# A delta rule, a PReLU MLP and a SwiGLU MLP on one core: a new order for the parts of gh, for the inverse products and for the decoding of weights

## The chip, the cores and the metric

One core of a Trainium2 chip. The time is the device time of one execution in microseconds (us): before, 1178.39, 1181.08 and 1181.10 us in three runs (median 1181.08). The profiled execution, from which all rows come, took 1177.41 us, with a span of 1175.7 us between its first and last instruction.

The engines are TensorE (PE in the rows, its weight loads PEld), VectorE (DVE), ScalarE (ACT), GpSimd (POOL) and SyncE (SP), which issues the DMAs.

## What is computed

```python
# attention: q, k, v (4, 8, 768, 48), beta (4, 8, 768)
k_n = k / (norm(k) + 1e-06)
for t in range(768):
    y[t]  = q[t] @ state
    v_old = state @ k_n[t]
    state = state + beta[t] * outer(k_n[t], v[t] - v_old)
x = y as (3072, 384)
# first MLP, PReLU
h = x @ w_in                                  # 384 -> 2048
g = maximum(h, 0) + alpha * minimum(h, 0)
x = g @ w_out                                 # 2048 -> 384
# second MLP, SwiGLU
out = (silu(x @ w_gate) * (x @ w_val)) @ w_out2   # 384 -> 1536 -> 384
```

Inputs and outputs are float32, but `w_in`, `w_out`, `w_gate` and `w_val` come as float64 and are read as 64-bit words.

## The kernel before

**Arithmetic.** Every large product is made in three passes: both factors are split into a high part (a copy in the fp32r format of TensorE) and a low part (the value less its high part), and high by high, high by low and low by high are summed. A high part is a copy by ScalarE; a low part is a subtraction on VectorE or GpSimd.

**Weights.** The 64-bit words of a slice of 128x384 weights are turned into float32 by four instructions: a scaled read of the upper words by ScalarE (`act`, tile `wf`, L518), and three bit operations on VectorE (`dve(0)` to `dve(2)`, L526, L528, L532). Then `split` makes the high part on ScalarE (L539) and the low part (L540). The first MLP has 32 slices, 16 of `w_in` and 16 of `w_out` by turns; the generator `all_w1` (called `conv`) decodes them, three steps for each slice, during the prelude and the first block. In its order, slice i+1 is read by ScalarE ahead of the bit operations of slice i, and both parts of slice i-1 are made at the second step of slice i. Odd slices have their low part on VectorE, even ones on GpSimd. `wf` has three buffers.

**Attention.** The 768 positions are 24 chunks of 32, in 6 windows of 4 chunks, with all 32 heads together. A window needs the inverse of a triangular 32x32 matrix for each head and chunk, in two halves of 16 (`lanes` for the later windows, `lanes2` for the first; HC is 16): a long elimination on VectorE, then for each pair of chunks (z = 0 and 1) a product `out1(z)` (L342), a copy out of PSUM by ScalarE into `tmp`, a second product (L364) and a subtraction into `TT`. The recurrence over chunks has the steps QS, KS, U, S, Y and XT; XT turns a chunk's result into columns of x, `xh` and `xl`.

**First MLP.** 12 blocks (n) of 256 tokens, 16 hidden slices (j). `H1(n, j)` is nine matmuls (L599), then two relus on ScalarE (L609, L610, tile `pn`), the PReLU sum on VectorE (L612), the high part of g on ScalarE (L616, tile `gh`) and its low part on GpSimd (L617). `O1(n, j)` is nine matmuls (L628) that add to a PSUM tile `o`; behind the last j of a block, ScalarE (L638) and VectorE (L643) copy `o` into `xs`, which goes to DRAM. `o` has one buffer, so that O1(n+1, 0) waits for these copies.

**Second MLP.** 8 blocks of 384 tokens (L686, L696 to L702, L715). Its weights are decoded early, stored in DRAM, and read again; their splits (`make_w2`), two in each step, and the first `split_x2` (L670, L671) lie in block 11 of the first MLP.

**Order.** Nothing is scheduled by a program: `manual_schedule` keeps the order in which the code is written. `prelude()` is straight code, in which `go(inv, k)` and `go(conv, k)` advance the inversion and the decoding by k steps. After it comes a list of events, each with a time u by which they are sorted; one unit is one H1. H1(n, j) is at 16n + j, O1(n, j) at 16n + j + 2.5. Each engine works its own instructions off in this order and waits where an operand isn't there or a buffer isn't free.

Of the kernel before, what the change touches and what calls it, by code (L numbers as in the profile page):

```python
# [13 lines left out]
AF = mybir.ActivationFunctionType  # L14
ALU = mybir.AluOpType
# [9 lines left out]
def kernel(  # L25
# [25 lines left out]
    nc = tc.nc  # L51
# [13 lines left out]
    NB1 = NCH // 2  # L65
    NB2 = NCH // CB2
    LA = 2
    W64 = 1
    WF = 3

    dram = ctx.enter_context(tc.tile_pool(name="dram", bufs=1, space=bass.MemoryType.DRAM))
    x2d = [dram.tile([128, 2, NK, 128], F32, name=f"x2d{n}") for n in range(NB1)]
# [2 lines left out]
    ws = ctx.enter_context(tc.tile_pool(name="ws", bufs=2 * J1))  # L75
# [169 lines left out]
    HC = C // 2  # L245
# [56 lines left out]
    def lanes2(w, early=False):  # L302


        t = Lanes(w)
        t.new_X()
        t.turn(0)
        yield
        t.turn(1)
        yield  # L310
        t.norm()
        t.length(0)
        yield
        Lv = free_view(t.L, 0, [[HC * C + HC, 2], [C, HC], [1, HC]])
        av = free_view(t.a, 0, [[HC, 2], [1, HC], [0, HC]])
        nc.vector.tensor_tensor(Lv, Lv, av, ALU.mult)
        yield
        tv = t.new("tmp", "tmp", [128, 512])
        B2 = [HC * C + HC, 2]
        for i in range(HC - 1):  # L320
            n, m = HC - 1 - i, i + 1
            v = free_view(tv, 0, [[n * m, 2], [m, n], [1, m]])
            Xv = free_view(t.X, (i + 1) * C, [B2, [C, n], [1, m]])
            Lc = free_view(t.L, (i + 1) * C + i, [B2, [C, n], [0, m]])
            Xr = free_view(t.X, i * C, [B2, [0, n], [1, m]])
            nc.vector.tensor_tensor(v, Lc, Xr, ALU.mult)
            t.length(2 * i + 1)
            nc.vector.tensor_tensor(Xv, Xv, v, ALU.subtract)
            t.length(2 * i + 2)
            yield  # L330
        Dm = t.new("Dm", "lane", [128, 32, C], 2)
        nc.gpsimd.memset(Dm[:, :, HC:C], 0.0)
        TT_t[w] = t.new("TT", "TT", [128, 32, C], 2)
        t.turn_X(1)
        G, TT = GL.pop(w), TT_t[w]
        ps = [None, None]

        def out1(z):
            ps[z] = bank(early, "pi")
            for y in range(HC * z, HC * z + HC):  # L340
                for b in range(4):
                    nc.tensor.matmul(  # L342
                        ps[z][rows(b), (y % HC) * HC:(y % HC) * HC + HC],
                        G[rows(b), y, :],
                        TT[rows(b), y, HC:C],
                        start=True,
                        stop=True,
                        skip_group_check=True,
                    )

        N = HC * HC
        uv = t.new("tmp", "tmp", [128, 512])
        t.turn_Dm(Dm)
        yield
        for z in range(2):
            out1(z)
            nc.scalar.activation(out=uv[:, z * N:z * N + N], in_=ps[z][:, 0:N], func=AF.Copy)
            if z == 0:
                t.turn_X(0)
            yield  # L360
            for y in range(HC * z, HC * z + HC):
                for b in range(4):
                    r = slice(32 * b, 32 * b + HC)
                    nc.tensor.matmul(  # L364
                        ps[z][rows(b), N + (y % HC) * HC:N + (y % HC) * HC + HC],
                        Dm[r, y, :],
                        uv[r, y * HC:y * HC + HC],
                        start=True,
                        stop=True,
                        skip_group_check=True,  # L370
                    )
            Tv = TT[:, HC * z:HC * z + HC, HC:C]
            nc.vector.tensor_tensor(
                Tv, Tv, ps[z][:, N:2 * N].rearrange("p (y i) -> p y i", y=HC), ALU.subtract
            )
            yield

    LANES2 = 4 + HC - 1 + 6
# [115 lines left out]
    class Slice:  # L494
# [8 lines left out]
        def load(self, eng=nc.sync):  # L503
# [3 lines left out]
            else:  # L507
                if self.home is None:
                    w = wstg.tile([128, 384], I64, name="w64", tag="w64", bufs=W64)
                else:  # L510
# [25 lines left out]
    def split(f, eng, pool, tag):  # L536

        t = pool.tile([128, 2, 384], F32R, name="w", tag=tag, **({} if pool is ws else dict(bufs=1)))
        nc.scalar.activation(out=t[:, 0], in_=f, func=AF.Copy)  # L539
        eng.tensor_tensor(t[:, 1], f, t[:, 0], ALU.subtract)  # L540
        return t

    def w_cols(w, j):
        return w[:, j * 128:j * 128 + 128].rearrange("(k p) f -> p k f", p=128)
# [4 lines left out]
    w1 = []  # L549
# [7 lines left out]
    w1_s = [w1_slice(i) for i in range(2 * J1)]  # L557

    w2 = {}
    w2_order = [(j, z) for j in range(J2) for z in range(3)]  # L560
    w2d, w2_s = {}, {}
# [20 lines left out]

    def make_w2(i):
        pool, tag = (ws, "w") if i < 2 * J1 else (P2["x"], f"w{i}")
        w2[w2_order[i]] = split(w2_s.pop(i), nc.gpsimd if i % 2 else nc.vector, pool, tag)

    PASSES = ((0, 0), (0, 1), (1, 0))

# [1 line left out]
    g1_t, o1_t = {}, {}  # L590

    def H1(n, j):
        ps = ps_h1.tile([128, 512], F32, name="h1", tag="h1")
        w = w1[2 * j]
        x = x1_t[n]
        i = 0
        for kk in range(NK):
            for a, b in PASSES:
                nc.tensor.matmul(  # L599
                    ps[:, 0:N1],  # L600
                    w[:, a, kk * 128:kk * 128 + 128],
                    x[b][:, kk, :],
                    start=(i == 0),
                    stop=(i == 3 * NK - 1),
                )
                i += 1
        hv = ps[:, 0:N1]
        pn = g1.tile([128, 2, N1], F32, name="pn", tag="pn", bufs=2)
        nc.scalar.activation(out=pn[:, 1], in_=hv, func=AF.Relu, scale=-1.0)  # L609
        nc.scalar.activation(out=pn[:, 0], in_=hv, func=AF.Relu)  # L610
        g = pn[:, 0]
        nc.vector.scalar_tensor_tensor(  # L612
            out=g, in0=pn[:, 1], scalar=nalpha[:, j:j + 1], in1=pn[:, 0], op0=ALU.mult, op1=ALU.add
        )
        gh = g1.tile([128, 2, N1], F32R, name="gh", tag="gh", bufs=3)
        nc.scalar.activation(out=gh[:, 0], in_=g, func=AF.Copy)  # L616
        nc.gpsimd.tensor_tensor(gh[:, 1], g, gh[:, 0], ALU.subtract)  # L617
        g1_t[n, j] = gh
# [45 lines left out]
    def split_x2(n):  # L664
        r = x2r_t.pop(n).rearrange("p c k t -> p k c t")
        t = P2["x"].tile([128, 2, NK, N2], F32R, name="x2s", tag="x2s")
        hv = t[:, 0].rearrange("p k (c t) -> p k c t", c=CB2)
        lv = t[:, 1].rearrange("p k (c t) -> p k c t", c=CB2)
        for kk in range(NK):
            nc.scalar.activation(out=hv[:, kk], in_=r[:, kk], func=AF.Copy)  # L670
            nc.gpsimd.tensor_tensor(lv[:, kk], r[:, kk], hv[:, kk], ALU.subtract)  # L671
        x2_t[n] = t

    u2_t, o2_t = {}, {}
# [61 lines left out]
    def at(u, fn, *args):  # L736
        events.append((u, len(events), fn, args))
# [10 lines left out]
    def load_w1(*slices, eng=nc.sync):  # L748
        for i in slices:
            w1_s[i].load(eng)  # L750

    def all_w1():

        n = 2 * J1
        w1_s[0].act()
        for i in range(n):
            if i + 1 < n:
                w1_s[i + 1].act()
            for z in range(3):
                w1_s[i].dve(z)  # L760
                if z == 1 and i > 0:
                    make_w1(i - 1)
                yield
        make_w1(n - 1)
        yield

    def make_w1(i):
        w1.append(split(w1_s[i].f, nc.vector if i % 2 else nc.gpsimd, ws, "w"))

    conv = all_w1()  # L770

    def go(g, n=1):
        for _ in range(n):
            next(g, None)
# [4 lines left out]
    def prelude():  # L779
# [10 lines left out]
        for g in range(4):  # L790
            m = mask[32 * g:32 * g + 32, :]
            nc.gpsimd.affine_select(
                out=m, in_=m, pattern=[[1, C]], compare_op=ALU.is_gt, fill=0.0, base=0, channel_multiplier=-1
            )
        load_nat(0, "k", nat)
        load_w1(0, 1)
        load_beta(0, nc.gpsimd)
        load_v(0, nc.gpsimd)
        load_v(1, nc.gpsimd)
# [1 line left out]
        n = 0  # L801
# [2 lines left out]
                pre_T(0, "k", b1, half, nat, early=n % 2 == 1, eng="act" if n % 2 == 0 else "dve")  # L804
                n += 1
        load_nat(0, "q", natq0)
        load_w1(2, 3)
        load_nat(1, "k", nat)
        nc.sync.dma_start(out=alpha_r, in_=moe_alpha.rearrange("(j p) -> j p", p=128))
        load_k2(0)  # L810
# [6 lines left out]
        inv = lanes2(0, True)  # L817
        go(inv, 3)
        n = 0
# [56 lines left out]
    def base(c):  # L876
        return {4: 20, 5: 25.7}.get(c, 8 * (c - 2))

    CONV_DONE, CONV_END = 41, 14.0
    CONV_N = 3 * 2 * J1 + 1 - CONV_DONE  # L880
    for i in range(CONV_N):
        at(-0.5 + i * CONV_END / CONV_N, go, conv)
# [1 line left out]
    for w in range(1, NWIN):  # L884
        P = base(4 * w) - 32
        if w == 1:
# [4 lines left out]
            l0, l1, n = 6.6, 18.5, LANES  # L891
        else:
# [9 lines left out]
            l0, l1, n = P + 15, P + 31.5, LANES  # L902
# [22 lines left out]
    for n in range(NB1):  # L925
        for j in range(J1):
            at(16 * n + j, H1, n, j)
            at(16 * n + j + LA + 0.5, O1, n, j)
    if WIDE2:
        NW2 = len(w2_order)  # L930

# [30 lines left out]
    for i in late:  # L962
        at(E1 - 16 + 3 + i / 2, fetch_w2, i)
        at(E1 - 16 + 5.1 + i / 2, make_w2, i)
    at(E1 + LA + 0.6, end1)
    for n in range(NB2):
        u = E1 + LA + 1 + J2 * n
        at(max(u - 10, E1 - 1.1) if n else E1 - 10, load_x2, n)
# [39 lines left out]
```

## Time and profile before

| | |
|---|---|
| runs | 1178.39, 1181.08, 1181.10 us |
| profiled execution | 1177.41 us (span 1175.7 us) |
| TensorE busy | 1087.1 us, 92% of the span |
| VectorE busy | 621.9 us, 53% |
| ScalarE busy | 444.4 us, 38% |
| GpSimd busy | 330.4 us, 28% |
| HBM traffic | 57.52 MB read, 16.52 MB written, 63 GB/s |

The span has these stages: the prelude with the first chunks of the recurrence, up to the first relu of H1(0, 0) at 73.8 us; block 0 of the first MLP with the rest of the weight decoding, up to 157.4; blocks 1 to 10, up to 665.3; block 11, up to 712; and the second MLP, up to the end. The average share of each engine hides that different engines are full in different stages, so the rows are read stage by stage. In a row of the timeline the number in brackets at the end is how long the engine was idle just before, and what ended it; "issue" is time in which it waited for nothing that the profile shows. A start is counted from the span's start. Matmuls overlap in part, so that a group's time is a little longer than the distance to the next.

### The profile page before, as it was taken

Reading aid. Unit: us, or ns where it says so; the run is one execution under the profiler, and the core shown is the slowest. Engines: PE = TensorE matmul, PEld = TensorE weight load, DVE = VectorE, ACT = ScalarE, POOL = GpSimd, SP = SyncE. Lnnn points to the kernel's source line nnn. Section 1 sums busy time; section 2 is a strip of 40 time slices with the busy share of each in tenths; the row PEclk is TensorE's granted clock in tenths of the full one; section 3 lists DMA queues with packets and bytes.
Section 4 is the critical chain, followed back from the end, with each engine's and each line's share of the span. In section 5 each row is a group of like instructions: output and inputs, shape, how many; then the busy total and the mean of one; then the engine's idle time right before and its main releaser. Section 6 shows DMA issues by size and latency. Waiting matters only on the chain.

```text
span 1175.7 us, 37218 instructions
## 1 busy us (share of the span) xinstructions
PE 1087.1 (92%) x16125; PEld 1049.6 (89%) x16125; DVE 621.9 (53%) x1313; ACT 444.4 (38%) x1158; POOL 330.4 (28%) x517
## 2 busy tenths in 40 slices
PE   6678689899999999999999989999999999999996
PEld 5567689889989998998899979999999999999996
DVE  6578963794497379449744255333333333333332
ACT  3254344335435543543444564222222222222221
POOL 4133732463274246327433373101010101001000
PEclk8579779999999999999999999999999999999998
DMA  9562021234224323422222153010101010101000
GB/s 224 166 203 44 2 68 39 76 83 123 57 82 107 86 74 83 119 61 70 78 76 76 56 155 101 1 42 1 41 1 41 1 41 1 41 4 38 11 11 20
DMA packets 140080, 76.44 MB, mean 65 GB/s; under 512 B 104000, under 2 KB 134624, under 8 KB 139916
## 3 DMA queue, kind: packets, MB, share of 16 engines
q1 hardware_dynamic: 139340, 73.45, 22.9%
q8 instruction: 126, 2.06, 0.7%
q0 software_dynamic: 576, 0.61, 0.2%
q14 instruction: 38, 0.31, 0.1%
HBM read 57.52 MB, written 16.52 MB: 63 GB/s over the span
## 4 chain that ended last, share of the span: by engine, by line
PE 60%; DVE 19%; issue 13%; ACT 3%; POOL 2%; DMA 1%; POOLq 0%; DVEq 0%; SPq 0%; ACTq 0%
PE gv L686 21%; PE o L715 10%; PE o L628 10%; PE h L599 10%; DVE tmp L257 4%; DVE pn L612 3%; DVE X L265 2%; PE pg L167 2%; DVE wf L532 1%; PE pt L148 1%; PE pst L444 1%; PE py L465 1%; DVE wf L528 1%; PE pk L400 1%; POOL w L540 1%
## 5 line engine op out<-in xcount | busy, mean ns | idle before, releaser
L686 PE MATMUL gv<-x2s,w 128*128 128x384 f32 x1728 | 317.8, 336 | 0.0
L686 PEld LDWEIGHTS gv<-x2s,w 128*128 128x128 f32 x1728 | 304.3, 188 | 0.0
L628 PE MATMUL o<-gh,w 128*128 128x256 f32 x1728 | 258.2, 293 | 22.8 <-POOL gh L617 9.6
L599 PE MATMUL h<-xh,w 128*128 128x256 f32 x1152 | 243.6, 288 | 12.7 <-ACT pn L610 6.7
L628 PEld LDWEIGHTS o<-gh,w 128*128 128x128 f32 x1728 | 223.1, 193 | 35.6 <-POOL gh L617 13.7
L617 POOL TENSOR_TENSOR gh<-pn,gh 128x256 fp32r<-128x256 f32 x192 | 151.7, 790 | 341.3 <-ACT gh L616 307.1
L599 PEld LDWEIGHTS h<-xh,w 128*128 128x128 f32 x1152 | 195.8, 194 | 15.7 <-ACT pn L610 7.3
L612 DVE SCALAR_TENSOR_TENSOR pn<-pn,nalpha 128x256 f32<-128x256 f32 x192 | 100.2, 522 | 150.6 <-ACT pn L610 149.5
L599 PE MATMUL h<-xl,w 128*128 128x256 f32 x576 | 165.3, 287 | 2.7 <-DVE xl L491 2.7
L715 PE MATMUL o<-w,us 128*128 128x384 f32 x864 | 165.4, 337 | 0.0
L616 ACT ACTIVATE gh<-pn 128x256 fp32r<-128x256 f32 x192 | 80.2, 418 | 220.0 <-DVE pn L612 220.0
L715 PEld LDWEIGHTS o<-w,us 128*128 128x128 f32 x864 | 151.2, 188 | 0.0
L698 DVE TENSOR_TENSOR sg<-sg,gv 128x384 f32<-128x384 f32 x96 | 53.2, 554 | 175.9 <-ACT sg L696 175.9
L671 POOL TENSOR_TENSOR x2s<-x2r,x2s 128x384 fp32r<-128x384 f32 x24 | 24.2, 1037 | 333.8 <-ACT x2s L670 333.8
L599 PEld LDWEIGHTS h<-xl,w 128*128 128x128 f32 x576 | 112.0, 194 | 4.0 <-DVE xl L491 4.0
L701 ACT ACTIVATE us<-u 128x384 fp32r<-128x384 f32 x96 | 50.6, 527 | 165.0 <-DVE u L699 165.0
L696 ACT ACTIVATE sg<-gv 128x384 f32<-128x384 f32 x96 | 47.2, 491 | 169.7 <-PE gv L686 169.7
L609 ACT ACTIVATE pn<-h 128x256 f32<-128x256 f32 x192 | 72.5, 377 | 90.7 <-PE h L599 87.7
L702 DVE TENSOR_TENSOR us<-u,us 128x384 fp32r<-128x384 f32 x96 | 53.7, 559 | 62.8 <-ACT us L701 62.8
L699 DVE TENSOR_TENSOR u<-sg,gv 128x384 f32<-128x384 f32 x96 | 53.2, 554 | 45.7 <-PE gv L686 45.5
L610 ACT ACTIVATE pn<-h 128x256 f32<-128x256 f32 x192 | 72.9, 380 | 0.0
L257 DVE TENSOR_TENSOR tmp<-L,X 128x31 f32<-128x31 f32 (+29 forms) x155 | 65.7, 424 | 1.4
(101 smaller groups left out, 1047.9 us busy)
## 6 DMA issues: line engine op xcount, KB each, us to landing
w<-in_moe_w_out_dram SPq DMA_DIRECT2D x28, 384.0 KB
w2d<-wf SPq DMA_DIRECT2D x36, 192.0 KB
wf<-w2d SPq DMA_DIRECT2D x36, 192.0 KB
w<-in_moe_w_in_dram SPq DMA_DIRECT2D x16, 384.0 KB
nat<-in_k_dram SPq DMA_DIRECT2D x24, 192.0 KB
k<-in_k_dram SPq DMA_DIRECT2D x96, 48.0 KB
x2d<-xs SPq DMA_DIRECT2D x12, 384.0 KB
w<-in_moe_w_gate_dram SPq DMA_DIRECT2D x12, 384.0 KB
```

The source lines that it names most:

```text
L257: eng.tensor_tensor(w, t.L[:, i + 1:C, i:i + 1].to_broadcast([128, n, m]), t.X[:, i:i + 1, c0:c0 + m].to_broadcast([128, n, m]), ALU.mult,)
L599: nc.tensor.matmul(ps[:, 0:N1], w[:, a, kk * 128:kk * 128 + 128], x[b][:, kk, :], start=(i == 0), stop=(i == 3 * NK - 1),)
L609: nc.scalar.activation(out=pn[:, 1], in_=hv, func=AF.Relu, scale=-1.0)
L610: nc.scalar.activation(out=pn[:, 0], in_=hv, func=AF.Relu)
L612: nc.vector.scalar_tensor_tensor(out=g, in0=pn[:, 1], scalar=nalpha[:, j:j + 1], in1=pn[:, 0], op0=ALU.mult, op1=ALU.add)
L616: nc.scalar.activation(out=gh[:, 0], in_=g, func=AF.Copy)
L617: nc.gpsimd.tensor_tensor(gh[:, 1], g, gh[:, 0], ALU.subtract)
L628: nc.tensor.matmul(o[:, dm // 2, (dm % 2) * N1:(dm % 2) * N1 + N1], w[:, a, dm * 128:dm * 128 + 128], g[:, b], start=(j == 0 and i == 0 an ...
L686: nc.tensor.matmul(p[:, 0:N2], w2[j, z][:, a, kk * 128:kk * 128 + 128], x[:, b, kk], start=(i == 0), stop=(i == 3 * NK - 1),)
L698: nc.vector.tensor_tensor(sg, sg, ps[0], ALU.mult)
L702: nc.vector.tensor_tensor(us[:, 1], u, us[:, 0], ALU.subtract)
L715: nc.tensor.matmul(o2_t[n][t][:, 0:DM], us[:, a, t * 128:t * 128 + 128], w[:, b, :], start=(j == 0 and i == 0), stop=(j == J2 - 1 and i == 2),
```

## The change

There are five edits.

1. `all_w1`: ScalarE's read `act` goes two slices ahead instead of one, so `wf` has four buffers. The high part of slice i-1 stands at the first step of slice i, the low part at the second (both stood at the second). Low parts of odd slices below 16 (`W1_DVE`) move from VectorE to GpSimd: eight subtractions. In the prelude the third weight load stands ahead of the load of q, not behind it.
2. `lanes2`: `tmp` is 256 wide and is allocated for each z, and the prelude's `go` counts list the second pair of chunks (z = 1) behind XT(1), both products, instead of its first product ahead of U(0).
3. H1 is cut in two: the high and low part of g (`H1_parts`) are listed at 16n + j + 0.45, half a step behind the relus and the sum.
4. O1(n, 0) of blocks 1 to 11 is listed at 16n + 3.1 instead of 16n + 2.5.
5. The low parts of the first `split_x2` (three subtractions) are on VectorE instead of GpSimd.

```diff
-        tv = t.new("tmp", "tmp", [128, 512])
+        tv = t.new("tmp", "tmp", [128, 256])
...
-        uv = t.new("tmp", "tmp", [128, 512])
...
             out1(z)
-            nc.scalar.activation(out=uv[:, z * N:z * N + N], in_=ps[z][:, 0:N], func=AF.Copy)
+            uv = t.new("tmp", "tmp", [128, N])
+            nc.scalar.activation(out=uv, in_=ps[z][:, 0:N], func=AF.Copy)
...
         nc.scalar.activation(out=t[:, 0], in_=f, func=AF.Copy)
-        eng.tensor_tensor(t[:, 1], f, t[:, 0], ALU.subtract)
-        return t
+        return t, lambda: eng.tensor_tensor(t[:, 1], f, t[:, 0], ALU.subtract)
...
+    def H1_parts(n, j):
+        g = g1_t[n, j]
         gh = g1.tile([128, 2, N1], F32R, name="gh", tag="gh", bufs=3)
         nc.scalar.activation(out=gh[:, 0], in_=g, func=AF.Copy)
...
-            nc.gpsimd.tensor_tensor(lv[:, kk], r[:, kk], hv[:, kk], ALU.subtract)
+            eng = nc.gpsimd if n else nc.vector
+            eng.tensor_tensor(lv[:, kk], r[:, kk], hv[:, kk], ALU.subtract)
...
         n = 2 * J1
-        w1_s[0].act()
-        for i in range(n):
-            if i + 1 < n:
-                w1_s[i + 1].act()
+        rest = None
+        for i in range(-2, n + 1):
+            if i + 2 < n:
+                w1_s[i + 2].act()
+            if i < 0:
+                continue
             for z in range(3):
-                w1_s[i].dve(z)
-                if z == 1 and i > 0:
-                    make_w1(i - 1)
-                yield
-        make_w1(n - 1)
-        yield
-
-    def make_w1(i):
-        w1.append(split(w1_s[i].f, nc.vector if i % 2 else nc.gpsimd, ws, "w"))
+                if i < n:
+                    w1_s[i].dve(z)
+                if z == 0 and i > 0:
+                    t, rest = split(w1_s[i - 1].f, nc.vector if i >= W1_DVE and i % 2 else nc.gpsimd, ws, "w")
+                    w1.append(t)
+                if z == 1 and rest:
+                    rest()
+                if i < n or z == 1:
+                    yield
...
-        load_w1(0, 1)
+        load_w1(0, 1, 2)
...
-        load_w1(2, 3)
+        load_w1(3)
...
-        go(inv, LANES2 - 13 - 4)
+        go(inv, 7)
         go(inv)
         go(conv, 4)
         go(inv)
-        go(conv, 2)
+        go(conv, 3)
         do_QS(0)
         do_U(0)
...
             at(16 * n + j, H1, n, j)
-            at(16 * n + j + LA + 0.5, O1, n, j)
+            at(16 * n + j + 0.45, H1_parts, n, j)
+            at(16 * n + j + LA + (1.1 if j == 0 and n > 0 else 0.5), O1, n, j)
```

What stands where on the engines, at the three places that matter most. First TensorE in the prelude, before, from the warm-up matmuls to chunk 0's part of the recurrence (L342 and L364 are the two products of the inverse, L426 is U, L444 is S, L400 and L465 are QS, KS and Y):

```order
L746 MATMUL warm<-ident 96x96 x6
L342 MATMUL pi<-TT,GL 32x16 x64
L364 MATMUL pi<-tmp,Dm 32x16 x64
L342 MATMUL pi<-TT,GL 32x16 x64
L426 MATMUL pu<-v,TT 32x48 x32
L444 MATMUL pst<-U,k_105 64x48 x32
L400 MATMUL pk<-St,kqt 32x48 x32
```

The same place in the changed kernel, where the numbers of lines are one higher:

```order
L752 MATMUL warm<-ident 96x96 x6
L343 MATMUL pi<-TT,GL 32x16 x64
L365 MATMUL pi<-tmp,Dm 32x16 x64
L427 MATMUL pu<-v,TT 32x48 x32
L445 MATMUL pst<-U,k_105 64x48 x32
L401 MATMUL pk<-St,kqt 32x48 x32
```

The second group of 64 first products is gone from the place ahead of U(0). Further down the same engine, around XT(1) (L487) and ahead of the transposes of q (L148) and the first H1 (L599), stood:

```order
L465 MATMUL py<-U,mt 32x48 x32
L444 MATMUL pst<-U,k_105 64x48 x32
L487 MATMUL px<-ident,ys 128x128 x3
L364 MATMUL pi<-tmp,Dm 32x16 x64
L148 MATMUL pt<-ident,nat_103 128x128 x8
L148 MATMUL pt<-ident,nat_104 128x128 x8
L599 MATMUL h_1334<-xh,w 128x256
```

and now, in the changed kernel:

```order
L466 MATMUL py<-U,mt 32x48 x32
L445 MATMUL pst<-U,k_105 64x48 x32
L488 MATMUL px<-ident,ys 128x128 x3
L343 MATMUL pi<-TT,GL 32x16 x64
L365 MATMUL pi<-tmp,Dm 32x16 x64
L149 MATMUL pt<-ident,nat_103 128x128 x8
L149 MATMUL pt<-ident,nat_104 128x128 x8
L600 MATMUL h_1337<-xh,w 128x256
```

The 64 first products came here, directly ahead of the second ones, with ScalarE's copy into `tmp` between the two. Third, ScalarE in block 11, before, two steps (relus of one H1, high part of g, high parts of two slices of the second MLP's weights):

```order
L609 ACTIVATE pn<-h_12572 128x256
L610 ACTIVATE pn<-h_12572 128x256
L616 ACTIVATE gh<-pn 128x256
L539 ACTIVATE w<-wf_12513 128x384
L539 ACTIVATE w<-wf_12527 128x384
L609 ACTIVATE pn<-h_12608 128x256
```

and in the changed kernel:

```order
L610 ACTIVATE pn<-h_12573 128x256
L611 ACTIVATE pn<-h_12573 128x256
L540 ACTIVATE w<-wf_12511 128x384
L621 ACTIVATE gh<-pn 128x256
L540 ACTIVATE w<-wf_12528 128x384
L610 ACTIVATE pn<-h_12609 128x256
```

One of the two weight copies moved from behind `gh` to between the relus and `gh`.

## Rows read from the trace of the kernel before

**Rows 1.** Windows by stage: us, busy and count by engine, PEclk, DMA share, GB/s
```profile
core 0: us, PE busy (x) PEld busy (x) DVE busy (x) ACT busy (x) POOL busy (x), PEclk, DMA share, GB/s
0.00:73.80 73.80, 45.69 (x1622) 40.83 (x1622) 46.74 (x117) 29.75 (x76) 20.79 (x37) 0.70 0.80 221
73.80:105.00 31.20, 28.98 (x718) 26.85 (x719) 23.30 (x47) 17.56 (x47) 10.70 (x12) 0.84 0.33 76
105.00:157.40 52.40, 35.47 (x473) 31.43 (x472) 49.41 (x109) 17.69 (x48) 30.86 (x57) 0.71 0.01 2
157.40:665.30 507.90, 485.20 (x10439) 461.42 (x10439) 310.16 (x710) 233.54 (x673) 210.56 (x353) 0.99 0.30 79
665.30:712.00 46.70, 39.09 (x288) 36.75 (x287) 25.07 (x32) 29.30 (x82) 31.31 (x33) 0.95 0.49 146
712.00:1175.70 463.70, 452.69 (x2593) 452.34 (x2591) 167.26 (x301) 116.60 (x237) 26.21 (x27) 0.99 0.07 23
```

**Rows 2.** Timeline of TensorE in the prelude: start, us, instructions, idle before
```profile
41.49 1.62 PE L342 MATMUL pi<-TT,GL 32*32 32x16 f32 x106 [4.29 <-issue]
...
63.60 1.78 PE L364 MATMUL pi<-tmp,Dm 16*32 16x16 f32 x116 [2.45 <-issue]
...
69.41 0.37 PE L599 MATMUL h<-xh,w 128*128 128x256 f32 x1
```

**Rows 3.** Timeline of the weight decoding on VectorE, ScalarE and POOL
```profile
50.87 0.99 POOL L540 TENSOR_TENSOR w<-wf,w 128x384 fp32r<-128x384 f32 x1 [5.80 <-ACT w L539]
50.88 1.40 DVE L532 SCALAR_TENSOR_TENSOR wf<-w,wf 128x384 int32<-128x384 int32 x1
51.90 0.55 ACT L518 ACTIVATE wf<-w 128x384 f32<-128x384 f32 x1 [1.10 <-POOL w L540]
...
73.89 0.56 DVE L540 TENSOR_TENSOR w<-wf,w 128x384 fp32r<-128x384 f32 x1 [1.88 <-ACT w L539]
74.83 0.55 DVE L532 SCALAR_TENSOR_TENSOR wf<-w,wf 128x384 int32<-128x384 int32 x1
```

**Rows 4.** Windows of two stretches of block 0, columns as in Rows 1
```profile
75.50:85.70 10.20, 9.13 (x163) 8.14 (x166) 7.15 (x15) 5.10 (x13) 4.57 (x5) 0.50 0.20 45
85.80:113.00 27.20, 24.38 (x641) 22.47 (x629) 21.70 (x42) 13.64 (x36) 9.40 (x11) 1.00 0.24 47
```

**Rows 5.** One block's window, TensorE's waits (157.4:712, then 575:712), one timeline row
```profile
318.00:356.00 38.00, 34.30 (x733) 32.31 (x732) 35.33 (x82) 14.39 (x43) 25.41 (x51) 1.00 0.37 96
...
PE o L628 <- DVE xs L643: 6.7, 9, 1.4
...
PE o L628 <- DVE xs L643: 1.9, 3, 1.3
...
327.82 1.32 PE L628 MATMUL o<-gh,w 128*128 128x256 f32 x9 [1.39 <-DVE xs L643]
```

**Rows 6.** Timeline of block 11, and ScalarE's waits there (total us, times, longest)
```profile
675.98 1.21 PE L628 MATMUL o<-gh,w 128*128 128x256 f32 x9
...
678.08 1.21 PE L628 MATMUL o<-gh,w 128*128 128x256 f32 x9
...
684.67 0.42 ACT L616 ACTIVATE gh<-pn 128x256 fp32r<-128x256 f32 x1 [1.04 <-DVE pn L612]
685.00 0.92 ACT L539 ACTIVATE w<-wf 128x384 fp32r<-128x384 f32 x2
686.00 1.19 POOL L540 TENSOR_TENSOR w<-wf,w 128x384 fp32r<-128x384 f32 x1
686.56 0.91 DVE L612 SCALAR_TENSOR_TENSOR pn<-pn,nalpha 128x256 f32<-128x256 f32 x1 [0.25 <-ACT pn L610]
687.50 0.42 ACT L616 ACTIVATE gh<-pn 128x256 fp32r<-128x256 f32 x1 [1.04 <-DVE pn L612]
...
694.34 3.49 POOL L671 TENSOR_TENSOR x2s<-x2r,x2s 128x384 fp32r<-128x384 f32 x3
...
699.84 1.87 PE L628 MATMUL o<-gh,w 128*128 128x256 f32 x8 [1.99 <-POOL gh L617]
...
ACT gh L616 <- DVE pn L612: 15.4, 16, 1.3
```

More of the change, by code (lines that the diff above doesn't have):

```diff
@@ L67 @@
     LA = 2
+    W1_DVE = 16
     W64 = 1
-    WF = 3
+    WF = 4
     dram = ctx.enter_context(tc.tile_pool(name="dram", bufs=1, space=bass.MemoryType.DRAM))
@@ L366, in lanes2 @@
                         Dm[r, y, :],
-                        uv[r, y * HC:y * HC + HC],
+                        uv[r, (y % HC) * HC:(y % HC) * HC + HC],
                         start=True,
@@ L584, in make_w2 @@
         pool, tag = (ws, "w") if i < 2 * J1 else (P2["x"], f"w{i}")
-        w2[w2_order[i]] = split(w2_s.pop(i), nc.gpsimd if i % 2 else nc.vector, pool, tag)
+        w2[w2_order[i]], rest = split(w2_s.pop(i), nc.gpsimd if i % 2 else nc.vector, pool, tag)
+        rest()
     PASSES = ((0, 0), (0, 1), (1, 0))
@@ L614, in H1 @@
         )
+        g1_t[n, j] = g
+    def H1_parts(n, j):
+        g = g1_t[n, j]
         gh = g1.tile([128, 2, N1], F32R, name="gh", tag="gh", bufs=3)
@@ L754, in all_w1 @@
         n = 2 * J1
-        w1_s[0].act()
-        for i in range(n):
-            if i + 1 < n:
-                w1_s[i + 1].act()
-            for z in range(3):
-                w1_s[i].dve(z)
-                if z == 1 and i > 0:
-                    make_w1(i - 1)
-                yield
-        make_w1(n - 1)
-        yield
-    def make_w1(i):
-        w1.append(split(w1_s[i].f, nc.vector if i % 2 else nc.gpsimd, ws, "w"))
+        rest = None
[4 more added lines that the diff above has]
+                continue
+            for z in range(3):
+                if i < n:
[4 more added lines that the diff above has]
+                if z == 1 and rest:
+                    rest()
+                if i < n or z == 1:
+                    yield
     conv = all_w1()
@@ L877, in base @@
         return {4: 20, 5: 25.7}.get(c, 8 * (c - 2))
-    CONV_DONE, CONV_END = 41, 14.0
+    CONV_DONE, CONV_END = 42, 14.0
     CONV_N = 3 * 2 * J1 + 1 - CONV_DONE
```

## The prediction

> **What bounds the kernel now.** I read the clock and busy time stage by stage first, then the chain of waits, then the stages in which TensorE waits. The table of windows [rows 1] is to be read by one question: which engine fills its stretch. The last 463.7 us (second MLP) have 452.69 us of TensorE work, and no edit reaches them. Blocks 1 to 10 of the first MLP (157.4 to 665.3) have 485.20 of 507.9: TensorE bound on the whole, with 22.7 us of waits. Three stretches are different: 0 to 73.8 (the recurrence of the first two chunks, TensorE 45.69, VectorE 46.74: a chain, nobody full), 105 to 157.4 (VectorE 49.41 of 52.4: VectorE bound), and block 11, 665.3 to 712 (TensorE 39.09 of 46.7; here ScalarE is in a loop with VectorE). The change can only win in those three and in the 22.7 us.
>
> **A. Prelude, 0 to 73.8.** Before, the products of the inverse for chunks 2 and 3 stand in front of U(0): 64 matmuls of 1.62 us, after TensorE had waited 4.29 us for nothing that the profile shows ("issue") [rows 2]. They now stand behind XT(1). So U(0) no longer has 1.62 us in front of it, and I let it win half of the stall, 2.1, since a stall that waits for nothing shown may fall on the next instructions instead: 3.8 us earlier for the chain U(0) to XT(1). What is late next: behind XT(1) now stand these 64 matmuls (1.62), a copy by ScalarE out of PSUM, for which the nearest row is ScalarE's other copies of 0.4 to 0.6 us [rows 3, 6], and then the second product (1.78, it stood there before too) [rows 2]. That gives back 1.62 + 0.6 = 2.2, so the first H1, whose matmuls start at 69.41 [rows 2], comes about 1.5 us earlier. The copy has company on its queue: reading weights two slices ahead, ScalarE goes round a loop in which it waits for POOL's subtraction (1.10 us idle, then the next read at 51.90, straight after POOL's 50.87 + 0.99) [rows 3]. Bounds: none of the stall won and the copy one loop of some 2 us late, 1.62 - 2.2 - 2.1 = -2.7; all of the stall won, 1.62 + 4.29 - 2.2 = +3.7. I take +1.5, nearer the middle. The third weight load, moved ahead of one load of q on SyncE's queue, stands before q's transposes: at the 221 GB/s of this stage [rows 1] its 0.39 MB are 1.8 us, which the 20% of the DMA time that is free and the inversion that runs meanwhile hide; if they don't, it falls under the -2.7.
>
> **B. Weight decoding, to 157.4.** Eight low-part subtractions of 0.56 us [rows 3] leave VectorE for POOL, 4.5 us in all. Six lie before 105, where TensorE is at work on half or full clock for 28.98 of 31.2 us [rows 1] and VectorE is not the bound: I count these as nothing, covered by TensorE. Two lie in the VectorE-bound stretch: 2 x 0.56 = 1.1, and I take +1. The trace has the counter-evidence in one pair of rows: a VectorE instruction of the decoding that takes 0.55 alone took 1.40 when POOL's subtraction ran from the same instant [rows 3]. Eight such meetings at 0.85 lost against 0.56 won would be 8 x -0.29 = -2.3, the lower bound; all eight wins on the path, +4.5, the upper. ScalarE's copies that read two slices ahead are 0.55 each as before and only earlier.
>
> [...]
>
> **C. Blocks 1 to 10: O1(n,0) one H1 later.** TensorE waits for the output copy xs of the block before, nine times, 6.7 us, at most 1.4 [rows 5]. Three of the nine lie after 575 and make 1.9 with a longest of 1.3 (block 11's, counted under D), so the ordinary small one is 0.3. Listed one H1 later, the wait is covered by a full H1, half of a step of 2.10 us [rows 6], 1.05. Of the eight left, 5.4 us, I take three as long (1.39 is the shown one) and five small, 5 x 0.3 = 1.5, all won. The long ones lie in blocks in which the window inversion runs: there VectorE has 35.33 of 38.0 us [rows 5], and a TensorE that no longer waits here waits for VectorE a step later, so I let each win 0.4: 1.2. C is 2.7; bounds 0 (everything given back to VectorE) and 5.4. The first parts of this edit, gh half a step behind pn, put ScalarE's copies of the recurrence ahead of gh; O1 follows H1 by two steps of at least 2.1, which hides half a step, so +0 here. If that cover is gone, a late low part on POOL costs TensorE what it costs at the worst place today, 1.99 [rows 6].
>
> **D. Block 11, 665.3 to 712.** Two slices of w_out are split in each step. ScalarE does gh, two copies (0.92), the two relus, and then waits 1.04 us for VectorE's pn before the next gh; gh to gh is 687.50 - 684.67 = 2.83, against 678.08 - 675.98 = 2.10 of TensorE's own step [rows 6]. With gh half a step later, one of the two copies falls between the relus and gh, into the 1.04. A copy is about 0.41 of the step, so the step is 2.42, still above TensorE's 2.10. The wait occurs 16 times, 15.4 us in all [rows 6]; eleven of the steps have copies to put there: 11 x 0.41 = 4.5. The three x2 low parts that leave POOL (3.49 there) for VectorE: they held a gh up until TensorE had waited 1.99 [rows 6]; VectorE, itself the wait of this loop, takes some 3 x 0.55 for them, so I take half, 1.0. The xs wait at this block's start: 1.05. D = 4.5 + 1.0 + 1.05 = 6.5. Bounds: the earlier copy makes POOL's subtraction meet pn more (0.91 beside 1.19 [rows 6]) and the 4.5 is lost, 2.0; all that TensorE is idle in the stage, 46.7 - 39.09 = 7.6.
>
> **Sum.** 1.5 + 1 + 2.7 + 6.5 = 11.7 us off the profiled execution, 1177.41 (its span 1175.7 and 1.7 around it): 1165.7. The other runs were 1178.39, 1181.08 and 1181.10, 1.0 to 3.7 above the profiled one; with 2.3 in between the forecast is 1168 us. The ends of A to D are -3.0 and +21.2 if all fall together; treated as independent, each half-width being about 3, some 6 to 7 about 11.7: 1161 to 1175 is the range of this case alone.
>
> **Rivals.**
> Hidden: gh waits for pn in all blocks anyway, and VectorE remains the clock of block 0, the lane blocks and block 11. Then C = 0, D = 2, A and B cancel: 1177.4 - 2 + 2.3 = 1178. For it: VectorE's 93% [rows 5] and its 49.41 of 52.4. Against: in block 11 VectorE is busy for 25.07 of 46.7 only [rows 1], so that a loop of waits and not an engine sets the step there.
>
> The other sign: TensorE's clock. It was granted 0.50 from 75.5 to 85.7 and 1.00 from 85.8 to 113 [rows 4], after a prelude with TensorE idle for over a third. If the new pause in front of H1(0) (the copy in ScalarE's queue) and small waits behind it keep the level at 0.50 up to 105, the 28.98 us of work there, of which 9.13 at half already, would have 19.85 doubled, less the 1.2 of idle time outside 75.5 to 85.7: +18.7, and 1168 becomes 1187. It decides when the clock does not come back by about 95: half of that price eats the forecast. Against it: the clock came back with the same mix of small waits before, and TensorE's share from 85.8 on is 24.38 of 27.2.
>
> More than forecast: the pause goes and the granted clock is 1.00 in 75.5 to 85.7 too: 9.13 / 2 = 4.6 more; with A and B at 3.7 and 3 (4.2 more) and D at 7.6 (1.1 more), 9.9: 1158.
>
> VectorE and POOL colliding eight times is no case of its own: -2.3 in place of +1 gives 1171, inside the range.
>
> **How the numbers follow.** Forecast 0.61, 1168; hidden 0.16, 1178; slower clock 0.10, 1187; more 0.13, 1158. The range for 8 in 10 takes in all of the forecast's range and most of "hidden", and a part of "more": 1157 to 1180. 0.3% of 1181.08 is 3.5 us, what a measurement here can tell from no change: faster is below 1177.5, slower above 1184.6. Faster: 0.13 + 0.59 + 0.05 of "hidden" = 0.77; same: 0.02 + 0.10 + 0.01 = 0.13; slower: 0.10.
>
> **What would show it.** A: U(0) starts 3 to 4 us before 43.1, where the 64 matmuls end now [rows 2], and H1(0)'s relu before 73.8; wrong if the wait before H1(0) is on ScalarE's tmp copy. B: the stretch from 105 to block 1 keeps VectorE above 90%; wrong if the decoding's VectorE instructions show more 1.4s. C: the nine xs waits gone; wrong if the same time stands as waits for gh at L628. D: ScalarE's wait before gh shrinks from 1.04 to about 0.6 and gh to gh is 2.4; wrong if it is 2.8. The forecast as a whole is wrong if block 11 and the first 157 us together are not at least 5 us shorter.

## The result, and the profile after

The changed kernel takes 1162.16 us (median of four runs, 1160.90 to 1165.26) against 1180.06 of the kernel before (four runs): a ratio of 0.9854, 95% interval 0.983 to 0.9878. The forecast was 1168, its range 1157 to 1180: the time lies inside, 6 us under the forecast. The profiled span went from 1175.7 to 1159.2 us, 16.5 less, where the terms had made 11.7. That the sum came out so near is in part luck: three of its four terms were far off, and two of the misses nearly cancel.

The windows by stage of the changed kernel, cut at the same events (first relu of H1(0,0), 105 us, first relu of blocks 1 and 11, start of the second MLP); columns as in [rows 1]:

```profile
0.00:80.20 80.20, 49.81 (x1612) 44.15 (x1616) 47.62 (x111) 30.34 (x77) 26.52 (x43) 0.64 0.78 217
80.20:105.00 24.80, 23.82 (x733) 22.00 (x721) 22.36 (x43) 16.49 (x44) 12.23 (x12) 1.00 0.27 52
105.00:156.20 51.20, 37.10 (x493) 33.08 (x492) 49.95 (x111) 18.91 (x50) 32.38 (x59) 0.73 0.01 2
156.20:654.40 498.20, 482.34 (x10425) 460.77 (x10425) 310.12 (x710) 234.90 (x673) 214.98 (x352) 0.99 0.31 81
654.40:695.50 41.10, 37.45 (x293) 35.27 (x292) 23.70 (x35) 29.38 (x82) 26.27 (x31) 0.98 0.56 169
695.50:1159.20 463.70, 453.22 (x2596) 452.88 (x2595) 167.51 (x302) 116.63 (x237) 26.43 (x27) 0.99 0.07 23
```

Against [rows 1]: the prelude is 6.4 us longer (73.8 to 80.2), block 0 is 7.6 shorter (83.6 to 76.0), blocks 1 to 10 are 9.7 shorter (507.9 to 498.2), block 11 is 5.6 shorter (46.7 to 41.1), and the second MLP is the same 463.7.

The prelude, TensorE's timeline: U(0) and XT(1) in the kernel before,

```profile
42.91 0.28 PE L426 MATMUL pu<-v,TT 32*32 32x48 f32 x3
...
45.60 1.17 PE L426 MATMUL pu<-v,TT 32*32 32x48 f32 x43 [2.02 <-issue]
...
60.37 0.55 PE L487 MATMUL px<-ident,ys 128*128 128x128 f32 x3 [0.66 <-ACT ys L474]
```

and in the changed kernel, in two pieces, U(0) and then from XT(1) to the first H1:

```profile
37.37 1.67 PE L365 MATMUL pi<-tmp,Dm 16*32 16x16 f32 x106 [1.11 <-issue]
39.63 0.69 PE L427 MATMUL pu<-v,TT 32*32 32x48 f32 x21 [0.58 <-DVE TT L374]
43.67 1.17 PE L427 MATMUL pu<-v,TT 32*32 32x48 f32 x43 [3.35 <-issue]
...
60.84 0.90 PE L488 MATMUL px<-ident,ys 128*128 128x128 f32 x3
...
64.22 1.78 PE L343 MATMUL pi<-TT,GL 32*32 32x16 f32 x115 [2.16 <-issue]
66.48 0.40 PE L365 MATMUL pi<-tmp,Dm 16*32 16x16 f32 x13 [0.47 <-ACT tmp L358]
69.05 1.78 PE L365 MATMUL pi<-tmp,Dm 16*32 16x16 f32 x115 [2.17 <-issue]
70.76 2.82 PE L149 MATMUL pt<-ident,nat 128*128 128x128 f32 x12
75.51 1.12 PE L149 MATMUL pt<-ident,nat 128*128 128x128 f32 x4 [1.92 <-issue]
76.27 0.56 PE L600 MATMUL h<-xh,w 128*128 128x256 f32 x1
```

U(0) does start earlier, 39.63 against 42.91, but after 21 matmuls the same kind of "issue" stall stands in front of the rest, and XT(1) comes no earlier than before. Behind it the two products meet a stall of 2.2 us each, of which the second product had one before too (2.45 [rows 2]), and q's transposes (L149) a new one of 1.92. The first H1 starts at 76.27 where it started at 69.41 [rows 2].

What TensorE waits for in blocks 1 to 11 (157 to 712), total us, times, longest:

```profile
PE o L633 <- POOL gh L622: 6.6, 17, 0.8
PE o L633 <- ACT gh L621: 5.4, 8, 1.3
...
PE o L633 <- DVE xs L648: 0.4, 1, 0.4
```

The xs waits of [rows 5], 6.7 us, are down to 0.4, and the waits for gh have not grown in their place. Block 11, two steps of ScalarE and what VectorE and POOL do in them:

```profile
671.71 0.42 ACT L621 ACTIVATE gh<-pn 128x256 fp32r<-128x256 f32 x1 [0.74 <-DVE pn L613]
672.04 0.51 ACT L540 ACTIVATE w<-wf 128x384 fp32r<-128x384 f32 x1
672.45 0.36 ACT L610 ACTIVATE pn<-h 128x256 f32<-128x256 f32 x1
672.72 0.37 ACT L611 ACTIVATE pn<-h 128x256 f32<-128x256 f32 x1
672.98 0.52 ACT L540 ACTIVATE w<-wf 128x384 fp32r<-128x384 f32 x1
674.24 0.42 ACT L621 ACTIVATE gh<-pn 128x256 fp32r<-128x256 f32 x1 [0.74 <-DVE pn L613]
...
672.91 1.01 POOL L541 TENSOR_TENSOR w<-wf,w 128x384 fp32r<-128x384 f32 x1
673.19 1.01 DVE L613 SCALAR_TENSOR_TENSOR pn<-pn,nalpha 128x256 f32<-128x256 f32 x1 [1.04 <-ACT pn L611]
```

gh to gh is 2.53, down from 2.83 [rows 6] and not the 2.42 forecast, since pn beside POOL's subtraction takes 1.01 where it took 0.91.

### The profile page after: what moved, and what is told of

The parts are those of the page before. It is cut to its first block, busy times and chain, and to the rows that moved or that the text cites. A ratio compares the mean times of both kernels' runs of the same rounds, so it can differ in the third digit from the quotient of the medians.

```text
span 1159.2 us, 37229 instructions
## 1 busy us (share of the span) xinstructions
PE 1083.7 (93%) x16125; PEld 1048.2 (90%) x16125; DVE 621.3 (54%) x1308; ACT 446.7 (39%) x1158; POOL 338.8 (29%) x522
## 4 chain that ended last, share of the span: by engine, by line
PE 64%; DVE 17%; issue 13%; POOL 3%; ACT 2%; DMA 1%; POOLq 0%; SPq 0%; DVEq 0%; ACTq 0%
PE gv L692 21%; PE o L633 12%; PE h L600 11%; PE o L721 10%; DVE tmp L258 3%; DVE pn L613 2%; DVE X L266 2%; POOL w L541 2%; PE pg L168 2%; DVE wf L533 2%; PE pst L445 2%; PE pt L149 1%; DVE wf L529 1%; PE pu L427 1%; PE py L466 1%
## 5 line engine op out<-in xcount | busy, mean ns | idle before, releaser
L633 PE MATMUL o<-gh,w 128*128 128x256 f32 x1728 | 256.2, 292 | 17.9 <-POOL gh L622 10.2
L613 DVE SCALAR_TENSOR_TENSOR pn<-pn,nalpha 128x256 f32<-128x256 f32 x192 | 105.9, 551 | 186.8 <-ACT pn L611 182.7
L677 POOL TENSOR_TENSOR x2s<-x2r,x2s 128x384 fp32r<-128x384 f32 x21 | 20.7, 1014 | 333.8 <-ACT x2s L675 333.8
```

What stands on the lines that cost most here:

```text
L613: nc.vector.scalar_tensor_tensor(out=g, in0=pn[:, 1], scalar=nalpha[:, j:j + 1], in1=pn[:, 0], op0=ALU.mult, op1=ALU.add)
L633: nc.tensor.matmul(o[:, dm // 2, (dm % 2) * N1:(dm % 2) * N1 + N1], w[:, a, dm * 128:dm * 128 + 128], g[:, b], start=(j == 0 and i == 0 an ...
```

## The experiments

Each ratio is to the kernel before, from runs on the same chip; "first relu" is that of H1(0,0), at 73.8 before, and "the first 15 steps" of block 11 run from the first relu of H1(11,0) to that of H1(11,15). Stage times come from one profiled execution of each kernel. In the four kernels that leave O1 and the high part of gh where they were (before, e3, e4, e9), blocks 1 to 10 take 507.9 to 508.8 us.

**e1, O1(n,0) alone, on the kernel before.**

```diff
-            at(16 * n + j + LA + 0.5, O1, n, j)
+            at(16 * n + j + LA + (1.1 if j == 0 and n > 0 else 0.5), O1, n, j)
```

> The kernel before with one edit: O1(n,0) listed one H1 later. Theory 1 (the prediction's term C): the nine xs waits, 6.7 us, go, but the long ones come back as waits for VectorE in the inversion blocks; blocks 1 to 10 are 2.7 us shorter, block 11 1.05, together 3.7. Theory 2 (every xs wait is on the path and is not given back): 5.4 + 1.3 = 6.7 us shorter. Theory 3 (this is where all the surplus of blocks 1 to 10 came from): about 9.7 + 1.

1176.2 us, 0.9982 (0.9965 to 0.9998). Blocks 1 to 10 took 509.6 us, not less than 507.9. TensorE's waits in them, and a window in block 7 (columns as in [rows 1]):

```profile
PE o L628 <- ACT gh L616: 5.7, 6, 1.4
...
PE o L628 <- POOL gh L617: 3.6, 9, 0.4
...
PE o L628 <- DVE xs L643: 0.2, 1, 0.2
```

```profile
518.40:521.60 3.20, 3.20 (x69) 2.98 (x71) 0.48 (x1) 0.77 (x3) 0.00 (x0) 0.50 0.01 1
```

The xs waits are gone (0.2), and yet this execution won nothing there. In the four blocks with a window inversion (2, 4, 6 and 8: 200.9 us against 199.4) the time is given back, as the prediction feared for the long waits. Of the other six, block 7 is 1.5 longer (53.8 to 55.3), and in it the granted clock was 0.50 as shown, where the kernel before had 1.00 from 219 to 665; the rest are 1.3 us shorter in sum. In e8 below, which has O1 with gh in its old place, the six take 305.1 us (308.5 before, 308.7 here). So whether O1 alone is worth something in blocks 1 to 10 is not settled. The start of block 11 won 1.2 us. Of the theories, 2 and 3 were too high; theory 1's 3.7 us (0.9969) lies inside the interval.

**e2, both parts of gh half a step later, alone.**

```diff
+        g1_t[n, j] = g
+
+    def H1_parts(n, j):
+        g = g1_t[n, j]
         gh = g1.tile([128, 2, N1], F32R, name="gh", tag="gh", bufs=3)
...
             at(16 * n + j, H1, n, j)
+            at(16 * n + j + 0.45, H1_parts, n, j)
```

> The kernel before with one edit: both parts of gh listed half a step behind pn. Theory 1 (the prediction): nothing in blocks 1 to 10, and block 11 4.5 us shorter, gh to gh 2.42 in place of 2.83. Theory 2 (ScalarE's copies of the recurrence, which no longer stand behind a gh that waits for pn, bring the recurrence forward): blocks 1 to 10 are 3 to 5 us shorter too, total 7.5 to 9.5. Theory 3 (half a step takes the cover of O1): blocks 1 to 10 longer, waits for POOL's gh above the 8.3 us of before.

1161.75 us, 0.9855 (0.982 to 0.9891): as much as the whole change, from this one edit, and about twice what theory 2 had; block 0 stood in no theory. Block 0 is 76.4 us (83.7 before), blocks 1 to 10 are 501.3 (507.9), block 11's first 15 steps 39.3 (41.9). Where it comes from is seen in block 0, ScalarE and VectorE of the kernel before:

```profile
105.53 0.38 ACT L610 ACTIVATE pn<-h 128x256 f32<-128x256 f32 x1
109.31 0.42 ACT L616 ACTIVATE gh<-pn 128x256 fp32r<-128x256 f32 x1 [3.41 <-DVE pn L612]
109.63 0.24 ACT L218 ACTIVATE sms<-L 128x32 f32<-128x32 f32 x1
109.78 0.53 ACT L518 ACTIVATE wf<-w 128x384 f32<-128x384 f32 x1
...
109.91 1.61 DVE L219 TENSOR_SCALAR smr<-sms 128x32 f32<-128x32 f32 x1 [0.63 <-ACT sms L218]
```

and the same place in e2:

```profile
102.05 0.38 ACT L610 ACTIVATE pn<-h 128x256 f32<-128x256 f32 x1
105.17 0.27 ACT L218 ACTIVATE sms<-L 128x32 f32<-128x32 f32 x1 [2.75 <-DVE L L203]
105.34 0.55 ACT L518 ACTIVATE wf<-w 128x384 f32<-128x384 f32 x1
106.00 0.42 ACT L620 ACTIVATE gh<-pn 128x256 fp32r<-128x256 f32 x1
...
105.89 0.17 DVE L219 TENSOR_SCALAR smr<-sms 128x32 f32<-128x32 f32 x1
```

Before, gh stood at the head of ScalarE's queue for 3.41 us, waiting for a pn that VectorE had not come to, and the inversion's square root (sms) and the next weight read stood behind it, the very things VectorE needed next: each engine waited for the other in turn. In e2 they go ahead of gh, which then has nothing to wait for; ScalarE waits 2.75 us at this place too, but with the instruction at its head that VectorE needs next. In the whole of block 0 VectorE waited 11.2 us for ScalarE before and 3.3 in e2. Over blocks 1 to 10 the waits of VectorE for ScalarE's copies say the same, before and in e2:

```profile
DVE pn L612 <- ACT pn L610: 138.4, 72, 4.2
DVE we L526 <- ACT wf L518: 17.1, 23, 1.5
DVE xs L643 <- ACT xs L638: 13.3, 10, 2.2
DVE mt L180 <- ACT GL L177: 11.5, 16, 1.1
```

```profile
DVE pn L612 <- ACT pn L610: 162.8, 81, 4.7
DVE xs L647 <- ACT xs L642: 7.5, 10, 1.2
DVE mt L180 <- ACT GL L177: 3.2, 14, 1.0
...
DVE we L526 <- ACT wf L518: 1.7, 4, 0.4
```

The 41.9 us of waits for copies (the last three rows) became 12.4, while the waits for the relus (first row) grew by 24.4: most of the time went there, and blocks 1 to 10 are 6.6 us shorter. The copy xs shows it on TensorE too, which waits for it

```profile
PE o L632 <- DVE xs L647: 1.2, 3, 0.5
```

where it was 5.4 us before, without O1 being moved. Where VectorE is full the waits lay on the path: the four inversion blocks 2, 4, 6 and 8 give 4.7 of the 6.6 (199.4 to 194.7). The other kernels agree: these four blocks take 199.0 to 200.9 us in the six with the high part of gh in its old place, 194.3 to 196.1 in the six with both parts at 0.45 there. That it is the copies behind gh is read from these rows; no run moves them and leaves gh.

**e8, the changed kernel with gh put back.**

```diff
-            at(16 * n + j + 0.45, H1_parts, n, j)
+            at(16 * n + j, H1_parts, n, j)
```

> The changed kernel with both parts of gh put back directly behind H1, all else as changed. Theory H (ScalarE's queue: a gh at the head of it waits for VectorE's pn, and all copies behind it wait too; half a step later these copies go ahead of it): this one edit carries the whole gain, so 1178 to 1181, with ScalarE's wait of gh for pn in block 0 back at about 28 us and block 0 at 82 or more. Theory S (the gains of single edits are shared, and the other edits carry it as well where gh does not): at most half is lost, 1165 to 1171. By the terms of the prediction alone (only block 11's 4.5 hangs on gh): 1166.7.

1177.04 us, 0.9995 (0.9982 to 1.0009): all other edits together are worth nothing that can be measured. Block 1 starts at 161.0, and ScalarE's waits of gh for pn in block 0 are back, 29.9 us in 16. Theory H holds; the prediction's own terms (1166.7) do not. Block 0 is 80.1 us here, 3.5 shorter than before without gh, but it also begins 7.1 later; the changed kernel's gh takes it from 80.1 to 76.0.

**e9, only the low part of gh half a step later** (the high part stays directly behind the relus).

```diff
-        nc.gpsimd.tensor_tensor(gh[:, 1], g, gh[:, 0], ALU.subtract)
-        g1_t[n, j] = gh
+        g1_t[n, j] = g, gh
+
+    def H1_low(n, j):
+        g, gh = g1_t[n, j]
+        nc.gpsimd.tensor_tensor(gh[:, 1], g, gh[:, 0], ALU.subtract)
+        g1_t[n, j] = gh
...
+            at(16 * n + j + 0.45, H1_low, n, j)
```

> The kernel before with only the low part of gh (POOL) half a step later; the high part (ScalarE) stays directly behind the relus. Theory H: nothing won, 1178 to 1181, since ScalarE's queue is as before. Rival P (it is POOL's queue, in which the low part stood ahead of the weights' subtractions and of the inversion's steps and waited): most of the 17 us of the whole edit, 1162 to 1168.

1172.66 us, 0.9958 (0.9944 to 0.9973): a third of the gain, between the two theories, so theory H alone falls short. But the third has one place: block 0 is 79.0 us (83.7 before), while blocks 1 to 10 stay at 507.9 and block 11's first 15 steps at 42.5. In block 0 POOL's queue, too, is held up by a gh that waits (27.4 us before, 17.9 here), with the weights' subtractions behind it; in the other blocks moving POOL's part alone won nothing.

**e3, the inverse order alone, and e4, the new decoding alone.**

```diff
-        go(inv, LANES2 - 13 - 4)
+        go(inv, 7)
```

> The kernel before with one edit: one advance of the inversion less ahead of U(0), so that both products of chunks 2 and 3 stand behind XT(1). Theory 1 (the prediction's term A): the first relu of H1(0,0) 1.5 us earlier than 73.8 and the total 1.5 shorter. Theory 2 (two code stalls and the half clock fall between XT(1) and H1, as the trace of the changed kernel has it): the first relu at 78 to 80, but block 1 starts within 1.5 us of 157.4, since VectorE and not TensorE sets the end of block 0; total within 1.5.

1178.37 us, 0.9988 (0.9974 to 1.0002); first relu at 79.8, block 1 at 159.9. Theory 2 has the late first relu and the unchanged total, though block 1 starts 2.5 later and not within 1.5; the gain of theory 1 did not come. e4 has the whole `all_w1` of the diff with its `split`, buffers and weight loads.

> The kernel before with the new decoding alone: reads two slices ahead, high and low part in different steps, eight low parts on POOL, four wf buffers, tmp 256 wide, third weight load ahead of q. Theory 1 (the prediction's term B): 1 us shorter up to block 1. Theory 2 (VectorE and POOL get in each other's way): VectorE's busy time up to block 1 is not 4.5 us less but about what it was (119.5), and block 1 starts within 1 us of 157.4 or later, to 160.

1181.24 us, 1.0022 (1.0005 to 1.0039); first relu at 78.2, block 1 at 160.6. VectorE's decoding, 32 slices up to block 1, before and in e4 (busy us, mean ns):

```profile
L532 DVE SCALAR_TENSOR_TENSOR wf<-w,wf 128x384 int32<-128x384 int32 x32 | 22.1, 690 | 0.4
L528 DVE SCALAR_TENSOR_TENSOR wf<-wf,we 128x384 int32<-128x384 int32 x32 | 20.2, 633 | 1.1
L540 DVE TENSOR_TENSOR w<-wf,w 128x384 fp32r<-128x384 f32 x16 | 9.3, 579 | 10.1 <-ACT w L539 10.1
```

```profile
L533 DVE SCALAR_TENSOR_TENSOR wf<-w,wf 128x384 int32<-128x384 int32 x32 | 23.9, 748 | 0.6
L529 DVE SCALAR_TENSOR_TENSOR wf<-wf,we 128x384 int32<-128x384 int32 x32 | 21.8, 682 | 1.1
L541 DVE TENSOR_TENSOR w<-wf,w 128x384 fp32r<-128x384 f32 x8 | 4.8, 595 | 0.0
```

The eight subtractions took 4.5 us with them, and 3.4 came back in the two shifts, which got longer: theory 2. Why they got longer, from 690 to 748 ns and from 633 to 682 in the mean, no run separates.

**e5, the changed kernel with the eight subtractions back on VectorE.**

```diff
-    W1_DVE = 16
+    W1_DVE = 0
```

> The changed kernel with the eight low parts of odd slices back on VectorE. Theory 1 (the prediction's B): 1 us slower, up to 4.5 at the worst. Theory 2 (each of POOL's subtractions lengthens one of VectorE's by up to 0.85): up to 2.3 us faster; VectorE's four decoding operations then take about 62 + 4.5 less what the meetings cost, 64 to 65 us up to block 1.

1163.21 us, 0.9877 (0.9863 to 0.9892), 1 us over the changed kernel and no clear difference: theory 1's size, not settled. Of VectorE's decoding the trace does settle something: up to block 1 its four instructions take 66.4 us here and 62.2 in the changed kernel, more than theory 2's 64 to 65. Beside a later gh, then, 5.0 us of subtractions were taken from VectorE and 1.4 came back in the shifts.

**e11, the changed kernel with the old inverse order** (e3's edit undone).

> The changed kernel with the inverse order of before (first product of chunks 2 and 3 ahead of U(0)), so gh, O1, x2 and the new decoding remain. It tells which of the two prelude edits takes the 4 us that the changed kernel (1162.2) is above the kernel with gh, O1 and x2 alone (1158.0). If the inverse order does (first relu of H1(0,0) 6 us later, and behind it VectorE no longer has the slack that absorbed it): 1158 to 1159 and the first relu before 77. If the decoding does: 1161 to 1163. The prediction's term A has it 1.5 slower without the edit: 1163.7.

1163.7 us, 0.9869 (0.9843 to 0.9895); first relu at 81.3 even so. Taking the inverse order back alone does not bring the prelude back, and the time is that of neither theory. All kernels with one or both prelude edits have the first relu at 78.2 to 81.3; the kernel before and those that keep its prelude have 73.8 to 77.4.

**e10, gh, O1 and x2 edits on the kernel before; prelude and decoding as before.**

> The kernel before with three edits: gh half a step later, O1(n,0) one H1 later, the first x2 low parts on VectorE; the prelude and the decoding stay as before. If the five edits add up as single ones measured (gh -17, O1 about -2, inverse order -0.3, decoding +2.6): about 1158 to 1160, 2 to 4 us under the changed kernel. If the new decoding pays only where gh no longer blocks ScalarE: 1163 or more.

1158.01 us, 0.9833 (0.9819 to 0.9848), first relu 74.8, blocks 1 to 10 498.2, block 11's first 15 steps 36.7. Beside gh, O1 is worth 3.1 us in blocks 1 to 10 (501.3 to 498.2). The time is what the single edits add up to by its expectation. The median is 4 us under the changed kernel; by the ratios 2.5, and the intervals overlap.

**e12 and e13, e10 with gh at 0.9 and at 1.2 of a step.**

> The kernel with gh, O1 and x2 edits (1158.0), gh at 0.9 of a step in place of 0.45. Theory H (copies stuck behind a waiting gh): a little more freed, 1156 to 1158, ScalarE's wait of gh for pn in blocks 1 to 10 below the 121 us of 0.45. Rival (the cover of O1 is used up already at half a step): slower, 1160 to 1165, TensorE's waits for gh above 8.1 us there.

> The same with gh at 1.2 of a step, behind the relus of the next H1: gh no longer waits for pn at all in most steps, but O1 has 1.3 steps of cover left. Theory H without a cover limit: 1152 to 1157. With the limit: TensorE waits for gh at L628's place in most steps, 1165 or more.

1162.76 us, 0.9866 (0.9828 to 0.9904), and 1170.13 us, 0.9922 (0.9891 to 0.9952): later is not better (at 0.9 the interval still overlaps that of e10). Blocks 1 to 10 lengthen from 498.2 to 504.3 and 507.1. The cover limit shows, but as a slope and not as waits in most steps: TensorE's waits for gh there go from 8.1 us to 11.1 and 12.7, which is only part of what these blocks lose; the rest is not traced. Block 11 is another matter: its first 15 steps take 33.4 at 0.9, since both copies now fall into the wait. Hence **e14**: 0.9 in block 11 alone.

```diff
-            at(16 * n + j + 0.45, H1_parts, n, j)
+            at(16 * n + j + (0.9 if n == NB1 - 1 else 0.45), H1_parts, n, j)
```

> The kernel with gh, O1 and x2 edits (1158.0), gh at 0.45 of a step in blocks 0 to 10 and at 0.9 in block 11 alone, where 0.9 brought the first 15 steps from 36.7 to 33.4. If both copies of weights then fall into ScalarE's wait for pn, and this stage is independent of the others: 3.3 us less, 1154 to 1156. If the gain is given back between block 11 and the second MLP: 1157 to 1159.

1156.9 us, 0.9814 (0.9785 to 0.9843), the fastest median of all kernels here. The first 15 steps of block 11 take 34.5 (36.7 in e10), so about a third of the 3.3 us was not kept; against e10 the intervals overlap.

The x2 edit has no run of its own; e2 and e10 differ by it and by O1 in block 11 (39.3 and 36.7 for the first 15 steps).

## Why the prediction was right, and where it was not

The time lay in the range and the sign was the forecast one. The step that failed stands in C: "The first parts of this edit, gh half a step behind pn, put ScalarE's copies of the recurrence ahead of gh; O1 follows H1 by two steps of at least 2.1, which hides half a step, so +0 here." It weighed only what a later gh costs O1, and not what it frees: e2 shows that gh alone is worth the whole 1.4%, e8 that all the rest is worth nothing measurable without it. So the time was forecast for other reasons than those that made it, and that it fell into the range is in part luck.

A. Wrong in sign. U(0) began 3.3 us earlier (42.91 to 39.63), near the forecast, but its second part only 1.9 (45.60 to 43.67) and XT(1) 0.5 later: of the stalls, of which half was to go, the 4.29 us ahead of it is gone, but the one in front of its second part grew from 2.02 to 3.35. "What is late next" was named rightly, the first product, the copy and the second product behind XT(1). The copy cost 0.47; what was missing were two new stalls, 2.16 in the first product and 1.92 in q's transposes, and a granted clock of 0.50 from 70 to 75 us, where it was 1.00 before. The stage is 6.4 longer, beyond the bound of -2.7, which took in no new stall. Some 2 us of this may be chance: 73.8 is the earliest of the eight kernels with the old prelude, whose mean is 75.8; the six with an edit in it have 80.2.

B. The stage from the first relu to block 1 is 7.6 shorter, but not by the decoding (e4: block 1 at 160.6): 4.1 of it is gh (e8 to the changed kernel, 80.1 to 76.0), and the rest goes with the later start, which e8 has too. VectorE's idle time in block 0 was 83.6 - 72.7 = 10.9 us before and 76.4 - 73.5 = 2.9 in e2. I had called the stretch VectorE bound from 105 on and not asked what VectorE waited for in the rest of the block. A and B together: -2.5 forecast, 6.4 - 7.6 = -1.2 measured.

C. 2.7 forecast, 9.7 measured, of which gh 6.6 (e2) and O1 3.1 beside it (e10). The price put on O1 came out about right, but not as it was counted: of the xs waits that it was counted from, gh alone had already taken 4.2 of 5.4 us (e2).

D. 6.5 forecast, 5.6 measured. The loop was read rightly; a step won 0.30 and not 0.41: with the earlier copy pn runs 0.73 us beside POOL's subtraction (672.91 + 1.01 - 673.19), where it was 0.63 [rows 6], and takes 1.01 instead of 0.91, the collision that had been put into the lower bound only. Of the first 15 steps' 5.2 us (41.9 to 36.7), gh gave 2.6 (e2), where 4.5 was forecast, and O1 and x2 together the other 2.6, where 2.05 was.

Rivals. The slower clock did not come behind the first relu: the granted clock from 80.2 to 105 is 1.00, where 0.84 was granted from 73.8 to 105 [rows 1]. That is the condition of "more than forecast", but the clock does not make the gain of block 0: e10 was granted 0.50 from 77.7 to 84.4 and starts block 1 at 153.4, e8 was granted 1.00 from 79.4 to 116.8 and starts it at 161.0. "Hidden" had the right reading, "gh waits for pn in all blocks anyway", and drew the wrong conclusion from it: the wait was there, and others stood behind it.

## What to carry to other kernels

When an instruction waits at the head of an in-order queue, do not ask only who waits for its result: list what stands behind it, and look whether the engine it waits for needs one of these. A wait that an edit takes away can also go by another edit (the xs waits, by O1 in e1 and by gh in e2); so try edits alone and by leaving one out, and do not read the worth of a small one from a single profile. And moving work from a full engine to a neighbour is to be booked with what the rest of the full engine's instructions then take: of 4.5 us moved, 3.4 came back in e4, and of 5.0 beside a later gh 1.4 (e5).

## What was not expected of the hardware

Several of TensorE's "issue" stalls in the prelude lie one count of matmuls apart. In the changed kernel's rows above, from one stall to the next there are 115 + 13 = 128 matmuls (64.22 to 69.05) and 115 + 12 = 127 (69.05 to 75.51); 106 + 21 = 127 from 37.37 to 43.67; before, 106 + 22 = 128 from 41.49 to 45.60. Not all do: before, 509 matmuls, four times about 127, lie between those at 45.60 and 63.60, and only 21 between two short ones, 0.55 and 0.56 us, ahead of 34.23 and 35.30. The 64 products that moved are 128 matmuls in the rows (13 + 115 behind XT(1)), one such count. With them gone from the place ahead of U(0), the 4.29 us there [rows 2] is gone too; but U(0)'s last 43 matmuls have a stall in front of them as before (2.02, now 3.35), and the moved products have one of 2.16 among them in their new place. What the engine lacks in them no run shows; "code stalls" in the expectation of e3 is a guess. One small VectorE instruction, `smr<-sms`, took 1.61 us before (at 109.91) and 0.17 in e2 (105.89) and in the changed kernel (112.00) at the same place of the program. In the first window, ahead of every gh, it took 0.67 before (17.73) and 1.47 in the changed kernel (18.47); no run here tells why. At this place in block 0 these 1.44 us are more than the 0.63 us for which VectorE waited.
